# Rewriting the first batch of an attention-and-MLP kernel: chunked loads, scores turned from the accumulator, activation in halves, and a written order on every engine

## The chip, the cores and the metric

The kernel runs on one core of a Trainium2 chip. The metric is device time in microseconds (us) of one execution. All runs quoted were in the fast state. In what follows, TensorE multiplies matrices, VectorE and ScalarE do elementwise work. PSUM is the accumulator memory that TensorE writes and the other two read. In profile lines PE is TensorE, DVE is VectorE, ACT is ScalarE, and L456 is line 456 of that kernel's own source (the two kernels have different line numbers).

## The reference, cut to what matters

```python
def _attn_ref(x, state):                      # x (8, 8, 512, 64), state (8, 8, 32, 64)
    scores = scale * np.matmul(x, state.transpose(0, 1, 3, 2))
    ...                                       # softmax over the 32 states: a
    xread = np.matmul(a, state)
    ...                                       # the same with the roles exchanged: sread
    return np.concatenate([xread, sread], axis=2)

def _moe_ref(x, w_in, w_out):                 # (4352, 512), (512, 2048), (2048, 512)
    h = x @ w_in
    sp = np.maximum(h, 0.0) + np.log1p(np.exp(-np.abs(h)))    # softplus
    g = h * erf(sp)
    return (g @ w_out).astype(np.float32)
```

The kernel never forms `xread`. It multiplies state by `w_in` first (the "mixed states" m, of 512 hidden columns per group, four groups per batch), and then attention weights by m. The weights arrive as 64-bit floats. They are fetched in sixteen pieces of one megabyte, and each piece takes two ScalarE and three VectorE operations to convert.

## The kernel before

Batch 0 is special. It runs while the weights are still being converted, in plain products. Batches 1 to 7 and a last one for the states use seven-product (Strassen) forms, and they keep TensorE full. For batch 0 each group goes: mixed states, four hidden products into PSUM banks, softplus by ScalarE and a copy of the hidden value by VectorE from the same bank, erf over the whole group, the gate product, and the output projection.

```python
def hidden(b, fts, copies=(nc.vector.tensor_copy,) * 4):
    ...
    for i, f in enumerate(fts):
        hp = ps_h.tile([P, S], F32, name="h")                # one PSUM bank of two
        ...                                                  # two matmuls into hp (L452)
        banks.append((nc.scalar.activation(out=s[:, i], in_=hp, func=ACTF.Softplus),  # L455
                      copies[i](hs[:, i], hp), on_pe))                                # L456

def finish(s, hs):
    return (nc.scalar.activation(out=s, in_=s, func=ACTF.Erf),       # L460, 128x2048 at once
            nc.vector.tensor_tensor(s, s, hs, op=ALU.mult))          # L461
```

Softplus and erf need different tables in ScalarE, and a load of a table (1.28 us in the traces) comes ahead of each switch. The order of instructions on each engine is left to a scheduler, which is guided by a few "issue after" marks. Batch 0 and batch 1 meet in these lines:

```python
        next(turn)                                           # softmax of batch 1
        prepare(1, begins(1), nc.scalar.copy)                # its mixed states and sums (L350 to L353)
        at = [combine_a(1)]                                  # sums of its weights (L381 to L384)
        behind([scored], lambda: done(project(gT_, g - 1, acc, range(2, NC))))
    ...
prepare(1, 1 - begins(1), nc.scalar.copy)
last = behind(at, combine_w)                                 # sums of w_out, 3 of 4 (L488)
```

## Time and profile before

The time is 755.34 us (755.03 to 757.14 over three runs). The stretches are set by events: the first output projection at 39.07 us, and the first seven-product projection at 142.23.

| stretch (us) | TensorE busy | what limits it |
|---|---|---|
| 0 to 39.07 | 34.5, of which 16.7 is warm-up | transfers, conversion, softmax in series |
| 39.07 to 142.20 | 98.37 of 103.13 | TensorE nearly full, VectorE 87.45 |
| 142.20 to 180 | 37.77 of 37.80 | TensorE |
| 180 to 720 | 539.38 of 540.00 | TensorE |
| 720 to 754.5 | 30.51 of 34.50 | the tail |

Read such a table from the bottom. Where TensorE is full nothing can be won without removing its work, so only the first 142 us are open. The prediction below shows these lines, the chain of waits and VectorE's waits.

One more view matters later: how softplus and hidden copy of one group stand to each other. The first fence is the timeline of ScalarE in the kernel before, the second that of VectorE, both for group 1. The columns are start, length, engine, line, operation, output<-input, shape and count; the bracket gives the idle time ahead of it and what ended it.

```profile
53.66 1.28 ACT L455 ACT_TABLE_LOAD   x1
54.95 1.09 ACT L455 ACTIVATE s<-h 128x512 f32<-128x512 f32 x2
```

```profile
55.55 1.23 DVE L129 SCALAR_TENSOR_TENSOR w_in<-raw,w_in 128x1024 uint32<-128x1024 uint32 x1
56.70 1.28 DVE L456 COPY hs<-h 128x512 f32<-128x512 f32 x2
```

The copies start after both softplus operations have ended, and they do not wait: VectorE was converting a weight piece until 56.70.

### The profile page before, as it was taken

To read this page: it belongs to the slowest core of one execution; us is meant where nothing else is said; L and a number is where in the kernel's file an instruction comes from. 1 tells how busy PE (TensorE), PEld (TensorE's weight loads), DVE (VectorE), ACT (ScalarE), POOL (GpSimd) and SP (SyncE) were. 2 spreads that over 40 slices of the span, in tenths; PEclk is the share of its full clock that TensorE was granted. 3 is DMA by queue.
4 is the path that set the end of the run, shared out by engine and by line. 5 is a ranking of instruction groups with operands and counts; after the bars stand their busy time and mean duration, and the time that the engine had idled before them with its cause. 6 is when DMAs were issued, how large, how long until landed. Compare 5 with 4: busy or idle time off the path is not lost.

```text
span 754.5 us, 12132 instructions
## 1 busy us (share of the span) xinstructions
PE 740.5 (98%) x5012; PEld 590.9 (78%) x5012; DVE 520.8 (69%) x774; ACT 381.1 (51%) x473; POOL 0.7 (0%) x6
## 2 busy tenths in 40 slices
PE   8998999999999999999999999999999999999997
PEld 7633434688888888888888888888888879999996
DVE  2888889786757666957687765766695865585523
ACT  5878863663455444554455445544455344443340
POOL 0000000000000000000000000000000000000000
PEclk9999999999999999999999999999999999999999
DMA  8565652241043001510061004300111000000001
GB/s 244 178 247 195 168 105 63 72 89 37 1 88 68 14 29 34 108 29 29 1 140 29 22 8 91 68 15 25 41 45 29 29 1 29 1 29 1 22 8 28
DMA packets 139230, 46.40 MB, mean 61 GB/s; under 512 B 126760, under 2 KB 130600, under 8 KB 139176
## 3 DMA queue, kind: packets, MB, share of 16 engines
q1 hardware_dynamic: 136776, 44.78, 23.5%
q10 hardware_dynamic: 2400, 0.85, 0.5%
q8 instruction: 39, 0.64, 0.4%
q14 instruction: 15, 0.12, 0.1%
HBM read 33.03 MB, written 8.91 MB: 56 GB/s over the span
## 4 chain that ended last, share of the span: by engine, by line
PE 81%; DVE 8%; ACT 2%; issue 1%
PE o L516 46%; PE h L410 25%; PE at L339 4%; PE o L466 3%; PE h L452 2%; DVE hs L418 1%; PE at L226 1%; DVE m L197 1%; DVE z L187 1%; PE at L177 1%; DVE raw L488 1%; ACT s L460 1%; DVE xT L303 1%; ACT L460 1%; DVE xT L190 0%
## 5 line engine op out<-in xcount | busy, mean ns | idle before, releaser
L461 DVE TENSOR_TENSOR s<-s,hs 128x2048 f32<-128x2048 f32 x34 | 77.9, 2292 | 72.0 <-ACT s L460 71.9
L417 ACT ACTIVATE s<-hs 128x512 f32<-128x512 f32 x120 | 75.5, 630 | 98.3 <-DVE hs L418 97.9
L516 PE MATMUL o<-w_out,s 128*128 128x256 f32 x480 | 119.1, 381 | 0.2 <-DVE s L461 0.2
L516 PE MATMUL o<-raw,hs 128*128 128x256 f32 x480 | 116.9, 384 | 0.0
L516 PE MATMUL o<-w_out,hs 128*128 128x256 f32 x480 | 114.8, 380 | 0.0
L516 PEld LDWEIGHTS o<-raw,hs 128*128 128x128 f32 x480 | 88.7, 190 | 30.9 <-issue 20.1
L516 PEld LDWEIGHTS o<-w_out,hs 128*128 128x128 f32 x480 | 90.4, 190 | 16.8 <-issue 4.2
L418 DVE TENSOR_TENSOR hs<-hs,h 128x512 f32<-128x512 f32 x90 | 61.4, 683 | 46.0 <-PE h L410 46.0
L516 PEld LDWEIGHTS o<-w_out,s 128*128 128x128 f32 x480 | 84.4, 191 | 9.7 <-DVE hs L418 0.8
L410 PEld LDWEIGHTS h<-aT,m 128*128 128x128 f32 x672 | 84.9, 192 | 8.4 <-issue 2.6
L410 PE MATMUL h<-aT,m 128*128 128x128 f32 x672 | 86.8, 276 | 0.4 <-DVE hs L418 0.4
L418 DVE TENSOR_TENSOR hs<-s,h 128x512 f32<-128x512 f32 x60 | 41.0, 683 | 42.9 <-PE h L410 42.6
L460 ACT ACTIVATE s<-s 128x2048 f32<-128x2048 f32 x34 | 65.0, 1911 | 0.4
L410 PE MATMUL h<-sy,sx 128*128 128x128 f32 x448 | 59.8, 276 | 1.6 <-DVE sy L382 1.2
L410 PEld LDWEIGHTS h<-sy,sx 128*128 128x128 f32 x448 | 56.6, 192 | 5.8 <-DVE hs L418 2.4
L426 ACT COPY hs<-h 128x512 f32<-128x512 f32 x30 | 17.4, 581 | 85.5 <-PE h L410 85.5
L466 PE MATMUL o<-w_out,s 128*128 128x512 f32 x128 | 58.6, 599 | 0.9 <-DVE s L461 0.9
L516 PE MATMUL o<-raw,s 128*128 128x256 f32 x240 | 57.6, 379 | 0.0
L421 ACT COPY s<-h 128x512 f32<-128x512 f32 x30 | 17.5, 582 | 72.1 <-PE h L410 71.6
L466 PEld LDWEIGHTS o<-w_out,s 128*128 128x128 f32 x128 | 23.3, 190 | 30.6 <-issue 29.4
L516 PEld LDWEIGHTS o<-raw,s 128*128 128x128 f32 x240 | 43.5, 190 | 4.7
L460 ACT ACT_TABLE_LOAD x34 | 43.6, 1283 | 0.6
(116 smaller groups left out, 887.9 us busy)
## 6 DMA issues: line engine op xcount, KB each, us to landing
raw<-in_moe_w_in_dram SPq DMA_DIRECT2D x8, 1024.0 KB, 5.3
raw<-in_moe_w_out_dram SPq DMA_DIRECT2D x8, 1024.0 KB, 4.8
x<-in_x_dram SPq DMA_DIRECT2D x60, 128.0 KB, 2.8
xq<-in_x_dram SPq DMA_DIRECT2D x112, 64.0 KB, 2.1
out_dram<-ot SPq DMA_DIRECT2D x18, 256.0 KB, 2.0
sc<-xT SPq DMA_DIRECT2D x112, 32.0 KB, 1.9
out_dram<-ot SPq DMA_DIRECT2D x28, 128.0 KB, 1.7
x<-in_x_dram ACTq DMA_DIRECT2D x4, 128.0 KB, 3.6
```

The source lines that it names most:

```text
L177: on_pe = nc.tensor.matmul(out=s2[e][q, :], lhsT=st[r, b, q], rhs=xT[r, i, :], start=True, stop=True)
L339: nc.tensor.matmul(out=ps[e][q, :], lhsT=st[r, b, q], rhs=w_in[r, fs, i, :], start=True, stop=True)
L410: last = nc.tensor.matmul(out=bank[:, q], lhsT=lhsT, rhs=rhs, start=(first and i == 0 and k == 0), stop=(i == GF - 1 and k == len(ops) - 1 ...
L417: nc.scalar.activation(out=s[:, k], in_=hs[:, k], func=ACTF.Softplus)
L418: add = lambda o, x, y: nc.vector.tensor_tensor(o, x, y, op=ALU.add)
L421: nc.scalar.copy(m1, p)
L426: nc.scalar.copy(c11, p)
L452: on_pe = nc.tensor.matmul(out=hp, lhsT=m_t[b, f // GF][:, e, P * (f % GF):P * (f % GF) + P], rhs=aT[b][:, e], start=(e == 0), stop=(e == 1))
L460: return (nc.scalar.activation(out=s, in_=s, func=ACTF.Erf), nc.vector.tensor_tensor(s, s, hs, op=ALU.mult))
L461: nc.vector.tensor_tensor(s, s, hs, op=ALU.mult))
L466: nc.tensor.matmul(out=acc[r], lhsT=gT[:, i, P * r:P * r + P], rhs=w_out[:, GF * g + i, :], start=(g == 0 and i == 0), stop=(g == NG - 1 a ...
L516: nc.tensor.matmul(out=acc[bank][:, E2 * c:E2 * c + E2], lhsT=lhs[:, i, :], rhs=rhs[:, g, i, :], start=(first and i == 0 and c == 0), stop ...
```

## The change

Its intent is to bring batch 0's first projection forward, and to close VectorE's gaps up to batch 1. The parts are these:

- x of batch 0 comes in four loads by chunk in place of eight by head; its turns go to four banks.
- VectorE turns the scores straight from PSUM, and the attention weights too, so TensorE's turns and their copies go. The warm-up before x is shorter.
- In groups 0 and 1, erf and the gate product are done in halves (in groups 2 and 3 in quarters), so the projection can start on the first half. This costs four more table loads.
- Every instruction of TensorE, VectorE, ScalarE and the transfer queue up to batch 1's sums is chained to the one written before it.

```diff
+    def in_order(begun):
+        last = {}
+        for i in nc.cur_bb.bb.instructions[begun:]:
+            if i.engine in last:
+                tc.add_manual_dep(i, last[i.engine].name, ..., reason="in_order")
+            ...
+            last[i.engine] = i
...
-    load_x(0, (nc.scalar, nc.sync))
+    for c in range(NC):
+        (nc.scalar, nc.sync)[c % 2].dma_start(
+            out=x_t[0][:, c], in_=x[0, :, P * c:P * c + P].rearrange("h p d -> p h d"))
...
-                on_pe = nc.tensor.transpose(out=s1[:, NI * c:NI * c + NI, :],
-                                            in_=sc[:, e, P * c:P * c + P], identity=ident)
+            nc.vector.transpose(out=both[:, e], in_=s2[e])
...
+    first0(0, 2, g0[0])
+    first0(0, 3, g0[0])
+    erf(A, g0)                    # A is the first half of the group
+    times(A, g0)
+    on_act("o", 1, [1])
+    for i in 2, 3:
+        soft(i, g0)
+        keep_h(i, g0)
+    erf(Z, g0)                    # Z is the second half
+    done(project(g0[0], 0, acc, range(NC), range(2)))
...
+    in_order(begun)
+    next(turn)
```

The rest of the diff writes out groups 1 to 3 and batch 1's softmax in the same manner. Batches 2 to 7 see only small edits.

## The prediction

> **What bounds the kernel now.** I first read the engines' busy time in stretches, to find where TensorE stops being short of work. Columns: stretch in us, its length, busy time (and instructions) of each engine, granted clock, DMA share, GB/s.
>
> ```profile
> 0.00:39.05 39.05, 34.51 (x228) 25.36 (x228) 22.63 (x32) 26.43 (x34) 0.70 (x6) 1.00 0.72 217
> 39.05:142.20 103.15, 98.37 (x450) 44.53 (x451) 87.47 (x109) 68.19 (x83) 0.00 (x0) 1.00 0.49 137
> 142.20:233.00 90.80, 90.77 (x702) 74.71 (x700) 68.48 (x111) 47.46 (x64) 0.00 (x0) 1.00 0.33 71
> 233.00:314.60 81.60, 81.50 (x593) 68.83 (x592) 58.27 (x95) 40.43 (x52) 0.00 (x0) 1.00 0.22 46
> ```
>
> From 142 us on TensorE is idle 0.03 us in 91, then 0.10 in 82: batches 1 to 8 are bound by TensorE, the diff removes none of its work there, and whatever is won before 142 us is won in the whole. Between 39.05 (the first output projection) and 142.20 TensorE is idle only 4.8 us, while VectorE is busy 87.5 of 103. Before 39.05 the busy figure deceives: 124 instructions are the warm-up on the identity, 16.7 us. Useful work there, by back-to-back durations, is about 16 us: 16 passes of the first product 6.9 (0.43 each), 16 turns of x 2.2, scores 1.2, turned scores and weights 2.4, mixed states 1.9, turned states 1.4. So 23 us of TensorE's time is lost before the first projection and 5 after it.
>
> Next the chain of waits up to 150 us, for what sets the moment at which TensorE is saturated for good.
>
> ```profile
> 102.28 1.92 ACT s L460
> ...
> 104.22 1.06 DVE s L461
> ...
> 106.43 1.30 DVE xT L299 x2
> 107.73 1.16 DVE m L302 x2
> 108.89 1.20 DVE xT L303 x2
> ...
> 120.33 0.34 DVE sy L384
> 120.67 2.20 DVE raw L488
> ...
> 127.48 2.20 DVE raw L488
> 129.68 0.61 DVE hs L418
> 130.28 0.04 issue
> 130.33 1.16 PE h L410 x8
> ```
>
> This is the view that decides my number. From 102 to 130 us the chain is VectorE without a gap: the gating product of group 3 (L461), the softmax of batch 1 (L299 to L308), its Strassen sums (L350 to L384), the sums of w_out (L488, four times 2.2 us), and only then the first sum of batch 1's hidden layer (L418). TensorE meanwhile had unfinished projections of batch 0 as filler. The two lines meet at 130: TensorE waits 0.4 us there. A change that brings only TensorE forward makes it wait here; VectorE's line must come forward too.
>
> Third, what VectorE waited for between 13.9 and 121 us:
>
> ```profile
> DVE m L262 <- PE at L259: 13.9, 1, 13.9
> DVE w_out L127 <- ACT w_out L125: 3.3, 3, 1.2
> DVE hs L456 <- ACT s L455: 3.1, 2, 2.1
> DVE s L461 <- ACT s L460: 2.8, 3, 1.8
> DVE z L201 <- ACT xT L199: 1.5, 1, 1.5
> DVE w_out L128 <- ACT raw L126: 1.1, 3, 0.4
> ```
>
> The first line is the start-up latency, the others are 11.8 us of gaps, most behind ScalarE. VectorE's content from 13.9 to the end of batch 1's sums (120.6) is thus 106.7 - 12 = about 94.7 us. No order can beat that.
>
> **What the Trainium skill says.** "ScalarE: Activation LUTs", What ACT_TABLE_LOAD costs: about 1283 ns a load plus a drain of some 1380 ns per switch. The trace agrees with the load (mean 1283 ns, 34 times with L460) and shows no such drain: the load at 53.66 takes 1.28 and the activation follows at 54.95. I charge 1.28. "VectorE: DVE Perf Modes", The three transpose paths: VectorE turns only 32x32 blocks. The scores' layout has 32-column blocks, and batches 1 to 7 already use this path (L299, 688 ns for 128x512); the source in PSUM is new, and no run so far shows it; I take the same 0.69. "DMA: Bandwidth & Descriptors", Anatomy of one DMA: a fixed 2 us or so per transfer. The x loads take 2.1 to 4.8 us to land, so it fits as a floor. "TensorE: Matmul & The Clock Gate", What's actually happening: half clock until some 3.4 us of activity. The warm-up agrees: its first 20 took 4.63 us (0.23 each), 24 later ones 2.84 (0.12).
>
> **The change part by part.** Durations below are back to back: a 512-wide VectorE operation 0.60, a 512-wide ScalarE copy 0.50, a weight piece 2.1 on ScalarE and, its three VectorE operations in sequence, 3.2 (0.81 + 1.26 + 1.15, from 53.48 to 56.70).
>
> Start-up. The same megabyte of x comes in four issues of 256 KB in place of eight of 128, so the last chunk lands at about the same time, near 8 us. Turns go into four banks, without waiting for copies, and the four copies are split between two engines: last copy near 9.9 instead of 11.4, scores done at 11.3 instead of 12.5. VectorE then reads the scores directly, at 11.3 against 13.9, but has one more 0.6 us operation per half. Turn, maximum, subtraction twice: 3.6, to 14.9. Piece i0: to 18. Two normalisations of about 1.9 and turns of 0.6: attention weights at 23.1 against 24.1. TensorE loses 8 + 8 turns (1.14 + 1.26 us) with their two copies.
>
> Group 0. First products 23.2 to 26.7; the second half of the mixed states needs piece i1 (VectorE 23.1 to 26.3) and ends, copied by ScalarE, at 28.2. Erf of the first half: load 1.28 and about 1.0, to 30.5; its product 1.2, to 31.8. First projection near 31.9 against 39.05: 7.1 us earlier, 1.2 of which are owed because the states of batches 1 to 7 are turned later. ScalarE pays four more table loads over groups 0 and 1 (5.1 us), and has room: 68 busy of 103.
>
> From there to batch 1's scores TensorE has in the written order: three mixed states 3, twelve first products of 1.72 = 20.6, projections of groups 0 to 2 at 13.75 = 41.3, states, turned weights and reading 3.5: 68.4 us. Dense, that puts the scores at 100.3. Walking both other engines along it I find gaps of about 0.3 before group 1's states, 0.8 and 1.3 before projections of groups 1 and 2 (table load, quarter erf, product), 2 where the turned weights wait for the banks of the mixed states: 4.5, so scores near 104.8. Before, they ran at 104.05. By then TensorE has 48 projections done instead of 40, which are 6.9 us of lead.
>
> VectorE: mixed copies to ScalarE -2.5, aT copies -1.2, xT copies +1.2 (before the scores), four turns +2.4, two more hidden copies +1.2, pieces of products +0.7, the turn of batch 1's weights (L310) moved behind the sums -1.2: about one us more or less, so again some 94 to 97 us, now begun at 11.3. With no gap the sums would end near 106; paced by TensorE's hidden products (copies wait for them) they end 13 us of softmax and sums after the scores are copied (+1): 115 dense, 119 with my gaps, against 120.6.
>
> The junction. After the sums come L310 (1.2, formerly before), combine 2.4 and w_out 6.6, so the first L418 starts at 125.5 to 129, against 129.68: 1 to 4 us won. TensorE's filler there shrinks from 16 whole projections (13.8 us) to about 6 (5.2 us): it will sit idle some 5 us. Not contending with filler, the five sums of the first hidden layer may take 4.6 instead of 5.6 us: 1 more. Sum: 2 to 5 us.
>
> **The rivals.** First, TensorE's lead counts in full: if the sums of the hidden layer overtake w_out's on VectorE, or the written order closes most of VectorE's gaps, 8 to 10 us go: 745 to 747. For it: the lead of 7 to 9 us is real by the sums above, and 11.8 us of gaps are there to be closed. Against it: the chain shows L488 three times before L418 although its product had ended near 121, and that code comes after the written order. Second, a fixed order has no slack: one late piece or table load stalls everything behind it, and pieces done in sequence pay 3.2 where interleaved ones pay 2.9 (16 x 0.3 = 4.8). Then nothing is won or a little lost: 755 to 758. For it: twelve new alternations between ScalarE and VectorE. Against it: ScalarE has a third of its time free. Third, transfers: early fetches of three weight pieces delay x by 1 to 2 us, and the 16 small loads of xq occupy the queue for 10 us just before the last pieces. I find the last piece landing near 90 with its use near 96, so hidden; if not, 2 us less.
>
> **Range and chances.** From 755.3 my walk gives 750 to 753.5; the first rival pulls down more strongly than the second pulls up, as whoever wrote the order will have looked at the gaps. I say 751, with 745.5 to 755.5 for 8 in 10. Faster by over 2% means below 740.2, 15 us: more than VectorE's gaps and start-up together (11.8 + 2.6), so 0.04. Slower by over 2% needs stalls of 15 us: 0.02.
>
> **What would show it.** First projection near 32; mean gaps of VectorE between 14 and 118 of about 10 us; batch 1's scores between 100 and 105; a TensorE gap of several us around 118 to 130, ended by VectorE's L418, which is new; from its first seven-product projection on the same 0.1 us of idle per batch. If TensorE has no gap there and VectorE reaches its sums before 112, my bound was wrong and the first rival holds. If batches 2 to 7 change their 81.6 us period, the small edits to their softmax matter and I missed it.

## The result and the profile after

The changed kernel took **761.20 us** (median of four runs, 759.09 to 761.28), and the kernel before 756.24 in the same rounds (755.03 to 757.18). The ratio is 1.006, with a 95% interval of 1.0034 to 1.0085. It is slower by about 0.6%, inside the class "within 2%", and outside the range on record (745.5 to 755.5). A ratio here is the mean time of one kernel's fast runs over that of the other's of the same rounds, so it is not quite the ratio of the medians quoted.

The busy time by stretches answers to the prediction's first fence. The columns are the same: the stretch, its length, then TensorE, its weight loads, VectorE, ScalarE, GpSimd, granted clock, DMA share, GB/s.

```profile
34.15:110.25 76.10, 70.52 (x271) 29.40 (x271) 59.56 (x70) 60.63 (x73) 0.00 (x0) 1.00 0.65 184
110.25:153.70 43.45, 37.70 (x287) 21.59 (x286) 37.24 (x52) 22.52 (x35) 0.00 (x0) 0.92 0.31 68
180.00:720.00 540.00, 539.86 (x3875) 464.38 (x3874) 371.54 (x568) 260.10 (x323) 0.00 (x0) 1.00 0.16 36
```

The first projection starts at 34.15 against 39.07, a real gain of 4.9 us. From 180 to 720 nothing has changed. All of the loss lies between. TensorE is idle 5.58 us up to batch 1's scores and 5.75 in the next 43 us. In that second stretch the granted clock is 0.92, and it was 1.00 throughout in the kernel before.

The whole reckoning in the profiled runs is this. From the first projection to the end the kernel before took 715.43 us (706.02 busy and 9.41 idle), and this one 724.55 (707.67 and 16.88). So idle time grew by 7.47 and busy time by 1.65, which is 9.12 lost against 4.92 won: 4.2 net, the difference of the spans (758.7 and 754.5).

The chain of waits answers to the prediction's second fence. Columns: start, length, what ran.

```profile
112.05 0.72 DVE xT L340
112.80 0.70 DVE m L343
113.52 0.69 DVE xT L344
...
117.77 1.53 ACT xT L230 x4
...
136.56 2.20 DVE raw L530
138.76 0.60 DVE hs L460
...
142.21 5.91 PE h L452 x32
```

It is the same chain in the same sequence, from the softmax of batch 1 to w_out's sums (L530) to the first hidden-layer sum (L460). It starts at 112.05 in place of 106.43, and L460 comes at 138.67 (in the timeline) in place of 129.60. Batch 1's scores themselves ran at 110.25; before they ran at 104.05, although TensorE had started its projections 4.9 us sooner. TensorE had finished 48 whole projections by then instead of 40. Its lead was spent on work for which nothing waited.

What VectorE waited for between 13 and 130 us answers to the third fence (who waited for whom: total us, times, longest).

```profile
DVE hs L679 <- ACT s L676: 11.9, 7, 3.5
DVE xT L294 <- PE at L198: 2.1, 1, 2.1
DVE z L232 <- ACT xT L230: 2.0, 2, 1.6
DVE s L685 <- ACT s L682: 1.2, 1, 1.2
```

The line to see is the first. The hidden copy (L679) waited 11.9 us behind softplus (L676); the same pair cost 3.1 before. The change meant to close VectorE's gaps, and it opened a larger one. The timeline of group 1, ScalarE first and then VectorE, shows one such wait, to be read beside the two fences of the kernel before:

```profile
52.13 1.28 ACT L676 ACT_TABLE_LOAD   x1
53.43 0.60 ACT L676 ACTIVATE s<-h 128x512 f32<-128x512 f32 x1
```

```profile
54.05 0.69 DVE L679 COPY hs<-h 128x512 f32<-128x512 f32 x1 [3.13 <-ACT s L676]
```

The copy begins when the softplus of its bank ends. That softplus stands behind a table load and, in ScalarE's written order, behind a weight piece (49.91 to 52.1). VectorE has other work, but the order puts it after the copy. The four long waits of this kind (1.57, 3.13, 1.80 and 3.51 us) all stand behind a table load and an operation or two of a weight piece.

Lastly, TensorE's timeline at the junction:

```profile
133.71 1.88 PE L508 MATMUL o<-w_out,s 128*128 128x512 f32 x4
139.41 1.82 PE L452 MATMUL h<-aT,m 128*128 128x128 f32 x8 [3.82 <-DVE hs L460]
142.21 2.08 PE L452 MATMUL h<-sy,m 128*128 128x128 f32 x8 [0.98 <-DVE hs L460]
```

The last projections of batch 0 end at about 135.6, then TensorE waits 3.82 us for VectorE. After that eight hidden products take 1.82, 2.08, 1.91 and 1.43 us, where eight take 1.05 at full clock: about 3.0 us more for the four groups.

### The profile page after: what moved, and what is told of

Its sections match the earlier page's. It is cut to its first block, busy times and chain, and to the rows that moved or that the text cites. A ratio compares the mean times of both kernels' runs of the same rounds, so it can differ in the third digit from the quotient of the medians.

```text
span 758.7 us, 11976 instructions
## 1 busy us (share of the span) xinstructions
PE 733.8 (97%) x4934; PEld 585.1 (77%) x4934; DVE 524.7 (69%) x775; ACT 390.4 (51%) x488; POOL 0.7 (0%) x6
## 3 DMA queue, kind: packets, MB, share of 16 engines
HBM read 33.03 MB, written 8.91 MB: 55 GB/s over the span
## 4 chain that ended last, share of the span: by engine, by line
PE 82%; DVE 6%; ACT 2%; issue 0%; DVEq 0%; ACTq 0%
PE o L558 47%; PE h L452 26%; PE at L381 3%; PE o L508 2%; PE h L672 1%; PE at L257 1%; DVE raw L530 1%; PE at L198 1%; DVE hs L460 0%; DVE aT L349 0%; DVE xT L344 0%; DVE xT L217 0%; DVE xT L340 0%; DVE m L343 0%; DVE m L222 0%
## 5 line engine op out<-in xcount | busy, mean ns | idle before, releaser
L503 DVE TENSOR_TENSOR s<-s,hs 128x2048 f32<-128x2048 f32 x30 | 68.8, 2292 | 68.4 <-ACT s L502 68.4
L460 DVE TENSOR_TENSOR hs<-hs,h 128x512 f32<-128x512 f32 x90 | 61.5, 684 | 46.6 <-PE h L452 46.6
L460 DVE TENSOR_TENSOR hs<-s,h 128x512 f32<-128x512 f32 x60 | 41.1, 685 | 42.0 <-PE h L452 41.4
L502 ACT ACTIVATE s<-s 128x2048 f32<-128x2048 f32 x30 | 57.3, 1911 | 0.3
L468 ACT COPY hs<-h 128x512 f32<-128x512 f32 x30 | 17.6, 587 | 77.0 <-PE h L452 77.0
L459 ACT ACT_TABLE_LOAD x32 | 41.1, 1283 | 0.6
```

Of the source, the lines that this page charges most:

```text
L459: nc.scalar.activation(out=s[:, k], in_=hs[:, k], func=ACTF.Softplus)
L460: add = lambda o, x, y: nc.vector.tensor_tensor(o, x, y, op=ALU.add)
L468: nc.scalar.copy(c11, p)
L502: return (nc.scalar.activation(out=s, in_=s, func=ACTF.Erf), nc.vector.tensor_tensor(s, s, hs, op=ALU.mult))
```

## The experiments

Three things could have eaten the gain, and the experiments began as a contest between them: the hidden copy behind softplus (A in the texts on record), the written order in batch 1's softmax (B), and the clock after the gap. Rivals added later were the amount of work on each engine by itself. "Over" is the median less the median of the kernel before in the same rounds. "Scores" is the start of batch 1's scores and "first sum" that of its hidden layer's first sum. All runs were fast, and correct unless said.

| kernel | median | over | ratio [95%] | scores | first sum |
|---|---|---|---|---|---|
| the change | 761.20 | +4.96 | 1.0060 [1.0034, 1.0085] | 110.25 | 138.67 |
| e1_copy_first | 766.17 | +10.62 | 1.0136 [1.0117, 1.0154] | 111.12 | 140.64 |
| e2_order_to_g3 | 757.46 | +1.91 | 1.0020 [1.0010, 1.0031] | 110.69 | 136.11 |
| e3_w_later | 756.40 | +0.85 | 1.0002 [0.9992, 1.0013] | 110.45 | 132.67 |
| e4_keep_warm | 758.30 | +2.75 | 1.0031 [1.0020, 1.0041] | 110.81 | 139.23 |
| e5_no_order | 764.52 | +7.72 | 1.0105 [1.0090, 1.0120] | 118.73 | 144.15 |
| e6_whole_erf | 775.40 | +19.86 | 1.0257 [1.0235, 1.0279] | 123.50 | 151.92 |
| e8_before_w_later | 754.12 | -1.42 | 0.9979 [0.9971, 0.9988] | 103.23 | 122.56 |
| e10_g3_w_later | 755.89 | +0.35 | 1.0000 [0.9990, 1.0011] | 110.44 | 133.65 |
| e11_st_first | 757.31 | +1.77 | 1.0016 [1.0007, 1.0025] | 112.48 | 135.69 |
| e12_before_startup | 756.59 | -0.21 | 1.0002 [0.9993, 1.0010] | 103.92 | 129.46 |
| e14_early_load | 755.91 | -0.89 | 0.9989 [0.9983, 0.9996] | 109.29 | 132.50 |
| e15_startup_w_later | 755.83 | -0.97 | 0.9995 [0.9987, 1.0004] | 104.10 | 123.43 |
| e16_less_tensor (wrong result) | 762.07 | +6.20 | 1.0086 [1.0061, 1.0110] | 111.47 | 139.89 |
| e17_less_vector (wrong result) | 761.57 | +5.70 | 1.0067 [1.0044, 1.0090] | 110.27 | 138.69 |
| e18_no_switch (wrong result) | 757.76 | +1.89 | 1.0022 [1.0011, 1.0033] | 105.50 | 133.93 |

One caution on the third and fourth digits of a start. Up to the first projection the granted clock varies from run to run (the means of 0 to 34 us lay between 0.90 and 1.00 for kernels with the same beginning), and it moves the first projection (33.0 to 34.5 us in the kernels that share that beginning). A few kernels (e2, e10, e11, e14) issue two of the sixteen scores early; the start given is that of the other fourteen. A difference of 1.2 us at the scores is therefore no finding.

### Is it the copy that waits behind softplus? (e1)

In all four groups the hidden copy is written before the softplus of the same bank.

```diff
-    soft(0, g1)
     keep_h(0, g1)
+    soft(0, g1)
     on_dve("o", 3, [0, 1])
-    soft(1, g1)
     keep_h(1, g1)
+    soft(1, g1)
```

> Only change: in batch 0's four groups VectorE's copy of a hidden bank is written before ScalarE's softplus of the same bank, so that softplus waits for the copy and not the copy for softplus and its table load. Theory A (the 11.9 us that VectorE spends waiting at these copies are the cause): the wait falls below 3 us, batch 1's scores move from 110.3 to about 105, the first hidden sum of batch 1 from 138.7 to about 133, and the time falls by 4 to 6 us to about 755 to 757. Rival theory B (the cause is the written order in batch 1's softmax, after the scores): the scores move, but TensorE paces them anyway and the time falls by less than 1.5 us.

It came out slower still, 10.62 over, which neither theory had. The waits of ScalarE and of VectorE in this kernel:

```profile
ACT s L676 <- DVE hs L679: 12.1, 8, 3.4
```

```profile
DVE s L685 <- ACT s L682: 8.9, 6, 2.6
```

The wait has changed sides. Softplus now waits 12.1 us for the copy, and the gate product (L685) 8.9 for erf. Two readers of one PSUM bank are evidently made to take turns, whichever is written first. "PSUM — Partial Sum Buffer" in the Trainium skill, PSUM bank collisions raise a hardware error, says why a program would be built so: two engines reading the same bank and quadrant at once is an error, and the compiler's scheduler adds a dependency between such instructions, ScalarE against VectorE too. The traces agree as far as they go: softplus and copy of one bank do not overlap in the fences shown. So A holds as a description of where the time is lost, but as a repair it falls. Hidden product, softplus, copy, erf, gate product and the next hidden product form a ring through three engines, and turning one link round does not shorten it.

### Is it the written order in batch 1's softmax? (e2)

The written order ends before batch 1's softmax, so the scheduler may interleave its two halves as in the kernel before.

```diff
+    in_order(begun)
     turn = attention(1, xT)
     next(turn)
...
-    in_order(begun)
     next(turn)
```

> The written order ends before batch 1's attention instead of after its sums; the scheduler interleaves the two halves of that softmax again. Theory B: the 17.6 us from the first turned score (112.05) to the end of the sums (129.66) shrink to about 14, and the time falls by about 3 us. Theory A: the stretch shrinks as well but it is the smaller part, under 3 us of time.

The time fell from 4.96 to 1.91 over. VectorE's timeline in this kernel:

```profile
112.48 1.30 DVE L340 STREAM_TRANSPOSE xT<-sc 128x512 f32<-128x512 f32 x2
113.70 1.24 DVE L343 TENSOR_REDUCE m<-xT 128x16 f32<-128x512 f32 x2
```

Two turns take 1.30 us together, and between each operation and the one that needs it stands another half's. In the changed kernel each operation stands right behind the one that it depends on, 0.72 to 0.75 apart (112.05, 112.80, 113.52 in the chain shown). From the first turn to the last of the sums this is 14.6 us here (112.48 to 127.09), 17.6 in the changed kernel (112.05 to 129.66) and 14.15 in the kernel before (106.43 to 120.58). Part of those 3 us is a wait of 1.64 us for exp's accumulated sum (L232), which the order places ahead of the normalisation. TensorE's gaps at the junction are 1.26 and 1.64 us, and eight products after each take 1.16. B is confirmed.

### Can the junction be relieved otherwise? (e3, e8, e10, e15)

In e3 the sums of w_out, 6.6 us of VectorE ahead of the hidden layer's, are moved behind batch 1's first hidden layer. The same edit is made to the kernel before (e8), to e2 (e10) and to e12 below (e15).

```diff
-    last = behind(at, combine_w)
+    last = None
...
             gT_ = first(lambda: next(steps))
+            if b == 1 and g == 0:
+                last = behind(at, combine_w)
             done(steps)
```

> The three sums of w_out for the seven-product projection are written after batch 1's first hidden layer, so that VectorE does the hidden sums between them. Theory D (TensorE is ahead at the junction and is only held by VectorE's order there, the first rival of the prediction): TensorE's 3.8 us gap near 136 to 139 vanishes, the cold clock after it too, and the time falls by 4 to 8 us. If the sums of w_out themselves bound the first projection, under 2 us.

> The kernel before with only the w_out sums written after batch 1's first hidden layer. There TensorE had 16 projections as filler and waited only 1.6 us at the junction, so by the account of the gap it gains at most 1.6 us: 754 to 755.5. If it gains 3 us or more, VectorE's order at the junction was worth more than the gap shows.

> The changed kernel with both repairs: the written order ends before batch 1's attention, and the w_out sums come after the first hidden layer. The first won about 3.7 us, the second about 4.8. If they act on the same gap of TensorE, the sum is about 5 us (756); if they add, 8 us (752.5 to 753), faster than the kernel before.

> The start-up of the change and the later w_out sums together on the kernel before. The later sums alone gave 754.1 against 755.5; if the two add, 753 to 753.5, the fastest so far; if TensorE is the bound after either, no better than 754.

In e3 the first sum comes at 132.67 in place of 138.67, TensorE's gaps shrink to 1.16, 1.59 and 0.41 us, and the time goes to 0.85 over. The gap thus cost up to 4 us, its cold clock included; the edit alone gains 1.4 where there is hardly a gap (e8). With e2's edit as well (e10) the result is 0.35 over, so the two do not add: they relieve the same gap.

On the kernel before, the edit gives 754.12 us over 18 runs, the fastest of all kernels here, and its interval (0.9971 to 0.9988) excludes no gain. It beats both the kernel before and the changed one. The timeline of TensorE in e8 at the point where the kernel before waited 0.38 us:

```profile
129.55 5.74 PE L466 MATMUL o<-w_out,s 128*128 128x512 f32 x13
```

TensorE runs through here, for the sum that it waited for has come at 122.56. But it waits elsewhere: from the first projection to the end its idle time is 9.3 us against 9.4. That stretch is 1.07 us shorter (752.4 - 38.04 against 715.43), and nearly all of it is busy time (705.0 against 706.0). So the gain is measured, and its cause is not a wait removed; fewer alternations between kinds of product would fit, but no run shows it. The start-up of the changed kernel adds nothing (e15: 0.97 under, e8: 1.42 under; the intervals overlap).

### What does the cold clock cost? (e4)

Sixteen identity products (32 instructions, 3.73 us) go in ahead of TensorE's last work before the gap (133.29 to 137.02), so that only 1.19 us of the gap are left.

```diff
         softplus(0)
         between()
+        if b == 1 and g == begins(1) and h == 0:
+            t = ps_at.tile([P, S], F32, name="at")
+            for _ in range(16):
+                nc.tensor.matmul(out=t[:, 0:P], lhsT=ident, rhs=ident, start=True, stop=True)
```

> 16 products of the identity (32 instructions, about 3.6 us) are put into TensorE's order just before its gap near 136 to 139; nothing else. Theory C (the gap cools the clock, and the matmuls of 139 to 148 run at half speed, 1.82 us for 8 instead of 1.05): the hidden products after the gap take about 1.05 us per 8 and the time falls by 2 to 4 us. If the slow matmuls lie beside a VectorE wait anyway: under 1 us.

Work that computes nothing makes the kernel faster: 2.75 over in place of 4.96. The two intervals overlap, so the verdict rests on TensorE's timeline of e4:

```profile
139.97 1.16 PE L452 MATMUL h<-aT,m 128*128 128x128 f32 x8 [1.19 <-DVE hs L460]
```

Eight products take 1.16 behind the wait and 1.06 later, where they took 1.43 to 2.08. The cold clock is worth 2 to 3 us of the loss.

### Is the written order to blame as a whole? (e5)

```diff
-    in_order(begun)
     next(turn)
```

> The changed kernel without the dependencies that hold the engines to the written order; all else as written, so the scheduler places the instructions as it sees fit. If the fixed order as such costs the time, this run is faster than the changed kernel by 3 us or more (below 758). If the order is needed to keep the halves of erf and the pieces in step, it is slower by 2 us or more.

No: without it the time is 7.72 over, worse than with it. The first projection comes only at 39.37, so the start's lead is gone. VectorE's wait at the hidden copies falls to 7.0 us, but TensorE then waits 8.6 us for those copies, and the scores come at 118.73. This emission of the instructions needs its order. The one part of it that was taken out alone, batch 1's softmax, does harm (e2).

### Are the halves to blame? (e6)

Erf of groups 0 and 1 goes back to one operation over the group, with the rest as in the changed kernel.

```diff
-    erf(A, g0)
-    times(A, g0)
...
-    erf(Z, g0)
+    erf(slice(0, 4), g0)
```

> Undoes one part: erf of groups 0 and 1 whole again, behind all four softplus (four table loads of 1.28 us less on ScalarE), the rest as in the changed kernel. Theory E (the extra table loads are what delays the hidden copies and with them VectorE): VectorE's wait at the hidden copies falls from 11.9 to about 7, the scores of batch 1 come 1 to 2 us earlier and the time falls by 1 to 2 us. Rival (the halves bring TensorE's projections forward and pay for their loads): first projection near 38.5 instead of 34.2, scores of batch 1 2 to 4 us later, the time grows by 2 to 4 us.

No: this is the slowest kernel, 19.86 over, where the theory expected a gain and its rival a loss of 2 to 4. VectorE's wait at the hidden copies grew to 26.2 us, where the theory said about 7. The first projection comes at 38.59, and TensorE waits 14.0 us for gate products, then runs cold (28 projection instructions in 15.02 us against 12.54). In the written order a group's projections stand right behind its own hidden products, so TensorE has nothing else to do while erf runs. The kernel before had projections of the previous group to run meanwhile (22 instructions from 76.78, during the erf of group 2). The halves are a repair that this order needs.

### Is the start-up worth anything alone? (e11, e12)

e12 puts the chunk loads, the four-bank turns and the turn from PSUM into the kernel before, with the shorter warm-up and VectorE's turn of the weights that go with them. e11 takes e10 and issues the two small state loads ahead of x, because they had landed late and held up the first table load.

```diff
-            s1 = ps_at.tile([P, NC * NI, Ns], F32, name="at")
-            ...                                             # TensorE turns the scores
+            nc.vector.transpose(out=both[:, e], in_=s2[e])  # e12, in the kernel before
```

```diff
+    for e in range(2):                                      # e11: ahead of the chunks
+        nc.sync.dma_start(out=st[:, 0, D * e:D * e + D],
+                          in_=state[0].rearrange("(i e) n d -> e i n d", e=2)[e])
     for c in range(NC):
         (nc.scalar, nc.sync)[c % 2].dma_start(
...
-        if c == 1:
-            for e in range(2): ...
```

> One part of the change alone, on the kernel before: x in four chunk loads, turned into four banks with copies on two engines, scores turned by VectorE from the accumulator; no written order, erf whole. My sums put the attention weights about 1 us earlier and take 2.4 us of turns off TensorE before the first projection: 0.5 to 1.5 us faster than the kernel before (754 to 755) if the start lies on VectorE's chain; no difference if the weight pieces set the pace.

> As e10_g3_w_later, and the two small state loads are issued before the x chunks instead of between them (they landed at 7.8 us and held ScalarE's first table load and half of the turns of x behind them). The turned state should be there near 6 us, the scores about 1 us earlier, the first turn of scores near 12 instead of 13. If the start-up lies on VectorE's chain to the junction, the time falls by about 1 us against e10; if TensorE's pace decides in between, by less than 0.5.

In e12 VectorE's first turn ran at 11.90, two us before VectorE had begun in the kernel before (13.91), but the first projection came at 38.38 against 39.07 and the scores at 103.92 against 104.05. The time did not move. In e11 the second x chunk landed later instead (TensorE waited 2.20 us for it), and the time rose from 0.35 to 1.77 over. Neither gave the gain hoped for: the start-up alone moves no end.

### Does a table load in idle time help? (e14)

A softplus of one column, written ahead of the copies of mixed states, draws the table load of groups 1 and 2 into time in which ScalarE is idle.

```diff
+    def early():
+        t = small.tile([P, 1], F32, name="early")
+        nc.scalar.activation(out=t, in_=ident[:, 0:1], func=ACTF.Softplus)
...
+    early()
     mixed(0, 1, copy=nc.scalar.copy)
```

> As e10_g3_w_later, with a one-column softplus written before ScalarE's copies of the mixed states of groups 1 and 2, so that the softplus table is loaded in ScalarE's idle time there (1.8 and 3.4 us) and not between a finished hidden product and its softplus. If the ring hidden product - table load - softplus - hidden copy paces groups 1 and 2, VectorE's wait at the hidden copies falls from 12.8 to about 10.5, batch 1's scores come 1.5 to 2.5 us earlier than 110.4, and the time falls by 1 to 2 us against e10. If the ring has slack, no difference.

It is built on e10, which stood 0.35 over; this stands 0.89 under. The wait at the hidden copies fell from 12.8 to 12.0 us, and the scores moved from 110.44 to 109.29. Part of that is the start (first projection 33.03 against 33.36). The intervals of the two kernels overlap and both movements fall short of the expectation (10.5 us, and 1.5 to 2.5 us earlier), so this decides nothing. In the profiled run half clock also set in at the junction (a granted clock of 0.55 from 138.83; two groups of eight products took 1.94 and 1.91), which may have hidden part of a gain.

### Which engine paces the stretch from 34 to 110 us? (e16, e17, e18)

This was still open: VectorE waits for ScalarE there, TensorE for both, ScalarE for TensorE. So each engine in turn was given less work. All three kernels give wrong results on purpose.

```diff
-    done(project(g0[0], 0, acc, range(3), range(2, 4)))       # e16: 3.4 us less for TensorE
+    done(project(g0[0], 0, acc, range(2, 3), range(2, 4)))
```

```diff
-            made[kind, j][1][k]()                             # e17: 6.4 us less for VectorE
+            if kind == "i" or j not in (2, 3):
+                made[kind, j][1][k]()
```

```diff
-        nc.scalar.activation(out=gT[0][:, ks], in_=gT[0][:, ks], func=ACTF.Erf)
+        nc.scalar.activation(out=gT[0][:, ks], in_=gT[0][:, ks],     # e18: 8 table loads less
+                             func=ACTF.Softplus if any(gT is t for t in (g0, g1)) else ACTF.Erf)
```

> Wrong result on purpose: four whole projections of group 0 (3.4 us of TensorE, 8 instructions) are left out of the changed kernel before group 1's mixed states. If TensorE's own work paces the stretch from the first projection to batch 1's scores, the scores come 3 us or more earlier than 110.3. If the weight pieces and the hidden copies pace it, TensorE only waits longer and the scores move by less than 1 us.

> Wrong result on purpose: VectorE's three operations on two weight pieces (w_out pieces 2 and 3, 6.4 us of VectorE) are left out of the changed kernel; ScalarE's part and the fetches stay. If VectorE's content paces the stretch, the scores come 5 us or more earlier than 110.3. If VectorE waits anyway at the hidden copies, its waits grow by most of the 6.4 us and the scores move by less than 2 us.

> Wrong result on purpose: erf of groups 0 and 1 is replaced by softplus, which takes as long but needs no switch of table, so eight loads of 1.28 us (10.3 us of ScalarE) vanish and nothing else changes. If the ring hidden product - softplus - erf - gate with its loads paces groups 0 to 2, VectorE's wait at the hidden copies falls from 11.9 to below 8 and the scores come 4 us or more earlier than 110.3. If the loads lie beside other work, under 1.5 us.

With 3.4 us less for TensorE the scores came at 111.47, no earlier. TensorE reached group 1's mixed states sooner and waited for a weight piece of VectorE's:

```profile
46.58 1.96 PE L381 MATMUL at<-w_in,st 64*32 64x512 f32 x16 [4.53 <-DVE w_in L150]
```

It ran cold after that (a granted clock of 0.50 to 0.54 up to 52.0). The mixed states start 13.63 us after the first projection, as they do in the changed kernel (47.78 less 34.15). So up to this point VectorE's conversion of the weights decides. With 6.4 us less for VectorE the scores came at 110.27, the same to 0.02 us, and the time freed reappeared as waiting. The work left out lies behind 47.55 in VectorE's line, so this says nothing of its work before that. VectorE's waits in e17:

```profile
DVE hs L680 <- ACT s L677: 16.3, 8, 6.4
```

With eight table loads less (8 x 1.283 = 10.3 us of ScalarE) the scores came at 105.50, 4.75 us earlier; the first projection of this run was 1.2 us early, so some 3.6 are the loads'. Of these, 1.4 are won before group 1's mixed states and the rest behind them. Net of the start, the expectation (4 us or more, and a wait below 8) is missed by a little on both counts. VectorE's waits in e18:

```profile
DVE hs L679 <- ACT s L676: 8.6, 5, 4.1
```

So the ring with its table switches delays batch 1's scores, by some 3.6 us. TensorE's work before 47.78 and VectorE's between 47.55 and 58 can be cut without moving them. Up to 47.78 VectorE's conversion sets the pace (e16), and what TensorE's work after 47.78 is worth was not tested; it is idle there for only 4.48 of 62.47 us. The size is to be kept in mind: 10.3 us of loads taken away gave 3.6 back. TensorE had only 5.58 us of idle time in the stretch, and 3.14 of 72.53 are left in e18.

## Why the prediction was wrong, point by point

**The bound was named rightly.** The prediction said that VectorE's line from batch 1's softmax to L418 decides, and that TensorE would sit idle at the junction until VectorE's hidden-layer sum. Exactly that wait appeared, ending at 139.41, as its largest: 3.82 us, or 4.8 with the one behind it, where "some 5" was said. It came later than said (from 135.6; "around 118 to 130"). Batches 2 to 7 kept their period, as said (scores 81.3 us apart, 81.6 before). One reading was off: L488 runs three times ahead of L418, not four; the walk itself charged three (6.6 us).

**Start-up: the mechanism right, the size two thirds.** It won 4.9 us of 7.1. The walk had the first projection near 31.9, and it came at 34.15. Turning scores from PSUM cost 0.71 to 0.72 us, as assumed (0.69). What was mis-sized was the term "scores done at 11.3": the state loads landed at 7.8 and held back a table load and half of x's turns, and the scores then took 2.83 us (1.83 in the kernel before, and 1.09 for the same sixteen at 110.25). They ended at 12.9. That is the pace of a cold clock, but the profile's granted clock reads 1.00 there, so it is not shown. The reading of the warm-up was loose in the same way: its first 20 products all took 0.23 each, up to 5.98, and so did the 16 turns of x behind them (3.62 us, up to 10.74), at a reading of 1.00. As e12 shows, a start like this counted for nothing at the end of the kernel before.

**The failed step** is the one worded "paced by TensorE's hidden products (copies wait for them)", with its companion that ScalarE "has room: 68 busy of 103". In the runs the copies wait for softplus, which shares their bank and stands behind a table load. The prediction's own third fence had the line that says so (3.1 us then), and it was passed over as a gap like others. Room on average says nothing about a ring: ScalarE's four extra loads (13 between 14 and 108 us, 9 before) lie between a hidden product and the next one that reuses its bank. The copies' wait grew from 3.1 to 11.9 us. All of VectorE's waits between 14 and 118 came to 15.0 us, where "about 10" was to show the prediction right. e18 prices the switches: without eight of them the stretch from the first projection to the scores takes 72.53 us, close to the walk's 72.9 (68.4 and 4.5 of gaps); with them it takes 76.10. Against the walk's 104.8 the scores came at 110.25. Of these 5.45 us, 2.25 are the later start, 1.1 more idle time (5.58 against 4.5) and 2.1 more busy time (70.52 against 68.4). The last probably stems from restarts after short waits (four first-product instructions take 1.98 us behind a wait, 1.72 dense), and in e18 the same 271 instructions are busy for only 69.39; no run separates it.

**The second failed term** is "13 us of softmax and sums after the scores are copied (+1)". It measured 17.6 from the first turn (e2: 14.6 without the written order there). The prediction had counted back-to-back durations, 0.60 each; but a fixed order of dependent neighbours runs at 0.72 to 0.75 each, and it waited 1.64 us for exp's accumulated sum. Also the turn of batch 1's weights stayed among the sums (L352, 125.27, behind the first of them), where the prediction had moved it behind them and taken 1.2 us off. The sums ended at 129.66, not at 115 to 119. Against 119 that is 5.45 us from the scores and 5.4 from here (19.4 us from the scores to the end of the sums, where 14 was said).

**A term was missing.** A gap of "some 5 us" was foreseen without its cost beyond itself. The page that the prediction cited for the warm-up, "TensorE: Matmul & The Clock Gate", says in the same place that an idle window throttles the clock again. The trace agrees: about 3.0 us in four groups of products, and e4 recovers 2.2.

**The rivals.** The first (the lead counts in full) fell: e3 and e10 put the hidden sums ahead of w_out's, which was its condition, and the time came only to 0.85 and 0.35 over. e16 shows that more lead early on only makes TensorE wait. The second (a fixed order has no slack; pieces in sequence pay 3.2) gave the right direction and was given too little weight, on the strength of ScalarE's average. Its reason also needs care: e5 shows the order to be worth 2.8 us to this kernel as a whole, and e2 shows that its last part costs 3. The third (transfers) played no part in the loss that the runs show.

**What stays open.** That softplus and the copy take turns because of their bank is inferred from e1's reversal and the skill's page; no run put them on different banks. The long waits stand behind a weight piece on ScalarE as well as behind a table load; e18 took the loads away, and no run moved the pieces. The run-to-run clock of the start-up was not controlled.

## What to carry to other kernels

Before adding work to an engine that "has room", follow one buffer round its whole ring, from the product that fills it to the next product that may refill it, and put the new work (here table loads) where the ring does not pass. Work done early counts only if something waits for it. When the order of instructions is fixed by hand, place independent operations between dependent ones, end the order where the scheduler does better, and keep TensorE's gaps few and short: half clock followed a gap of 1.44 us in one of these runs (e4, granted clock 0.56 from 24.96 to 28.80), though not every gap brought it.

## What the Trainium skill lacked or had wrong

- "ScalarE: Activation LUTs": the load of 1283 ns is confirmed (1.283 us, 32 times with softplus). The drain of some 1380 ns per switch does not show: the operation ahead of the load ended at 52.11, the load took from 52.13 to 53.41, and the activation began at 53.43.
- "TensorE: Matmul & The Clock Gate": its table of states puts the idle window at some 3.4 us (a later section speaks of short, frequent idle spells, without a length). In these runs half clock also followed gaps of 2.79 us (a granted clock of 0.57 from 20.62 to 24.20 in the changed kernel), 1.64 us (0.50 from 147.68 in e5, 0.55 from 138.83 in e14) and 1.44 us (0.56 from 24.96 in e4). A gap of 1.64 us in e2 and one of 3.08 us there (1.00 from 20.11 to 24.00) did no harm. So no length of gap separates the two here. In e17 the first eight products after a gap of 3.82 us still took 1.19 us and the next eight 2.08, so the throttle can come late.
- "VectorE: DVE Perf Modes", The DRAIN you can't avoid: it says that chaining operations without semaphores saves nothing, and that a next operation which is not held starts earlier, but not by how much. Here a 512-wide operation starts 0.72 to 0.75 us after one that feeds it, and 0.60 after one that does not.
- "VectorE: DVE Perf Modes", The three transpose paths: no figure for 32-bit data from PSUM. A 128x512 block took 0.71 to 0.72 us from PSUM and 0.70 to 0.71 from SBUF.
- "PSUM — Partial Sum Buffer": it warns of two readers of one bank but not of what taking turns costs in a pipeline: 11.9 us of waiting here, 12.1 with the order reversed.
